# A list scheduler sets the order of four engines in a fused attention and FFN kernel

## The chip, the core and the metric

The kernel runs on one core of one Trainium2 chip. The metric is the device time of one execution in microseconds (us). Every engine of the core (TensorE or PE, VectorE or DVE, ScalarE or ACT, GpSimd or POOL, and SyncE or SP, which issues transfers) takes its own instructions strictly in the order in which the program holds them; an instruction that waits for a semaphore holds back all that stand behind it on that engine.

## The reference

Attention with a threshold, then a bilinear feed-forward layer on its output. The float32 inputs q, k, v have 8 batches, 8 heads, 576 rows and 64 columns. The three weight matrices arrive as float64.

```python
scores = scale * np.matmul(q, k.transpose(0, 1, 3, 2))
thresh = np.max(scores, axis=-1, keepdims=True) - tau
scores = np.where(scores >= thresh, scores, -1000000000.0)
scores = scores - np.max(scores, axis=-1, keepdims=True)
attn = np.exp(scores)
attn = attn / (np.sum(attn, axis=-1, keepdims=True) + 1e-09)
out = np.matmul(attn, v)
...
a = x @ w_a        # x: 4608 x 512, from out; w_a, w_b: 512 x 1536
b = x @ w_b
return a * b @ w_out   # w_out: 1536 x 512
```

## The kernel before

**Tiling.** The work of attention is cut into 144 units, each of 128 rows of queries for a pair of heads. One unit does the following. `scores` (L404) makes two score tiles `sc` of 128x576 in PSUM on PE. On DVE two maxima `mx` (L411) and the threshold `thr` (L412) follow; ACT makes `bias` (L431) and the exponentials `tw` (L432); DVE cuts at the threshold and sums (L435), then takes the reciprocal (L446, L448); ACT scales (`normalise`, L454). The weights are then transposed. In the first 8 units (`BY_PE`) that is done on PE (L479, copied out by ACT L481 and DVE L482); later DVE transposes 32x32 blocks (L498 in `turn_blocks`, two instructions of 128x576 for a unit) and two transfers through DRAM (`swap`) put the blocks in place (`wT`). `product` (L542) multiplies with v into `pv`, and ACT L549 and DVE L550 copy that to the tiles `xT` of x, which POOL also copies with swapped halves (`xS`, L565).

The FFN works on blocks of 256 rows of x: products with `w_a` and `w_b` (`pab`, L824 and L720, partly by Strassen's seven products of sums and differences), their elementwise product `h`, sums of `h` on POOL (L853) and the products with `w_out` (`po`, L885; in the first block L935).

All PSUM tiles (`tp`, `sc`, `pv`, `pab`, `po`) come from one pool of 4 buffers, each of two banks.

**Weights.** In the first 140 us the float64 weights are loaded in 36 pieces (L271, SP's queue) and converted by integer steps: ACT L298 and L299, POOL L305, DVE L311 and L319, POOL L324. A piece's L311 is also the last to read the raw buffer, so that another piece can be loaded to it.

**What sets the order.** The Python text interleaves all of this: the loop over `g` (one unit each) calls `scores`, then the conversion of two or three pieces in portions (`convert_first`, `convert_rest`), `turn_blocks` of the unit before, `weigh`, `weighted`, and between them `advance`, which runs the FFN's matmuls for so many columns as a pace allows. `keep_order` then chains every engine's instructions in just this text order, by a dependency of each on the one before it (reason "order").

The transfers on SP are spread by `pump` and `load_weights`: a transfer waits for the PE instruction that stood last in the text when it was issued (reason "pace").

Of the kernel before, what the change touches and what calls it, by code (L numbers as in the profile page):

```python
# [35 lines left out]
TW_BUFS = 3  # L36
SEVENS = 2
BY_HEAD = 16


def keep_order(tc):

    last = {}
    for ins in tc.nc.cur_bb.bb.instructions:
        before = last.get(ins.engine)
        if before is not None:
            tc.add_manual_dep(
                ins, before,
                mybir.DependencyInfo(mybir.DependencyClass.NoSync, mybir.DependencyReason.DATA),
                reason="order")  # L50
        last[ins.engine] = ins.name


@with_exitstack
def kernel(
# [59 lines left out]
    INV_SCALE = math.sqrt(D)  # L115
    BIG = 3.0e38

    def pool(name, bufs, **kw):
        return ctx.enter_context(tc.tile_pool(name=name, bufs=bufs, **kw))

    const = pool("const", 1)
    loads = pool("loads", 3)
    work = pool("work", 2)
    small = pool("small", 2)
    scratch = pool("scratch", 5, space=bass.MemoryType.DRAM)
    psum = pool("psum", 4, space=PSUM)
# [37 lines left out]
    def flush(*keys):  # L164

        while any(key in keys for key, _, _ in bulk):
            pump(1, False)

    def passed(columns):

        running["pump"] += columns
        while bulk and running["pump"] >= 0:
            running["pump"] -= PUMP * sum(math.prod(to.shape) for to, _ in bulk[0][2]) // PART
            pump()
        if not bulk:
            running["pump"] = min(running["pump"], 0)
# [77 lines left out]
    def load_weights(limit, engine=nc.sync, most=NPIECES):  # L254

        behind = None
        if most < NPIECES:
            behind = next(x.name for x in reversed(nc.cur_bb.bb.instructions) if x.engine == mybir.EngineType.PE)
        while most and (len(raws) - len(taken) < limit or extra) and state["loaded"] < state["due"]:
            most -= 1  # L260
            n = state["loaded"]
            if len(raws) - len(taken) < limit:
                raw = work.tile([P, CW, 2], U32, tag="xT", bufs=XT_BUFS, name="raw")
            else:
                raw = taken[n] = extra.pop(0)
# [12 lines left out]
            state["loaded"] = n + 1  # L278
# [53 lines left out]
    for _ in range(TW_BUFS):  # L332
        t = work.tile([P, 2 * NB, Q], FP32, tag="tw", bufs=TW_BUFS, name="rows")
# [34 lines left out]
    def prep_pe(i, name):  # L368

        m = loaded[i][name]  # L370
        if name == "q":
            mT = first_sb[:, i * S:(i + 1) * S]
        else:
            mT = work.tile([P, S], FP32, tag="kT", bufs=HP, name="kT")
        tp = banks(SH, "tp")
        for c in range(2):
            for n in range(NR // 2):
                nc.tensor.transpose(tp[:, c, n * R:(n + 1) * R], m[:, c * (NR // 2) + n], ident[0:R, 0:R])
        prepared.setdefault(i, {})[name] = mT
        return mT, tp  # L380
# [8 lines left out]
    def scores(i, u):  # L389
# [566 lines left out]
    def store(n):  # L956

        for _ in range(n):
            post("out", pending.pop(0))
# [75 lines left out]
    first = {i: g for g, (i, u) in enumerate(units) if u == 0}  # L1035
# [3 lines left out]
    kT, tp = prep_pe(0, "k")  # L1039
# [17 lines left out]
    n = 0  # L1057
    for g in range(NPIECES):
        size = min(3 if 4 <= g < 10 else 2, NPIECES - n)
        early[g] = list(range(n, n + size))  # L1060
        n += size
    for g in range(len(units) + PV_LAG):
        written = len(pending)
        state["slot"], state["paced"] = g, g > 36
        while bulk and bulk[0][1] < g - 1:
            pump()
# [5 lines left out]
        if BY_PE + 1 < g <= len(units) + 1:  # L1072
            n = g - PV_LAG
# [152 lines left out]
```

## Time and profile before

| | |
|---|---|
| median of 3 runs | 1419.35 us (1418.83 to 1419.81) |
| span of the profiled execution | 1417.0 us |
| PE busy | 1370.2 us (97%) |
| DVE busy | 1013.7 us (72%) |
| ACT busy | 679.9 us (48%) |
| POOL busy | 495.7 us (35%) |
| longest chain | PE 86%, DVE 7%, DMA 3%, issue 2% |

The span goes from the first to the last instruction of the profiled execution; a time also holds what lies around the span. No time of the profiled execution itself is given beside its span, so the median stands for it: 2.35 us lie around the span. "Busy" is the union of an engine's instructions. Matmuls are pipelined, and one that has begun overlaps those that follow, so a busy PE may still wait a little.

### The profile page before, as it was taken

How to read it: one execution, taken by the hardware profiler on the slowest of the kernel's cores; microseconds unless marked ns; L12 is line 12 of the kernel's file. 1: busy time of each engine (PE TensorE's matmuls, PEld its weight loads, DVE VectorE, ACT ScalarE, POOL GpSimd, SP SyncE). 2: the span in 40 equal slices, each digit the busy share in tenths (PEclk: the TensorE clock that was granted, in tenths of full speed). 3: DMA queues.
4: the chain of work that ended last, by engine and by line, in shares of the span. 5: the costliest groups of instructions: out<-in, count | busy, mean ns of one | idle time of the engine just before them, and what ended most of it. 6: DMA issues, size and time to landing. Idle time of an engine off the chain costs nothing.

```text
span 1417.0 us, 76257 instructions
## 1 busy us (share of the span) xinstructions
PE 1370.2 (97%) x33836; PEld 1229.6 (87%) x33836; DVE 1013.7 (72%) x2200; ACT 679.9 (48%) x1245; POOL 495.7 (35%) x678
## 2 busy tenths in 40 slices
PE   6788999999999999999999999999999999999998
PEld 5677579989878887979998999999888899799997
DVE  6898986778777877776767777677777776744424
ACT  5786554545445454545444545454545455431110
POOL 2674541606060606042333324150606060608100
PEclk9999999999999999999999999999999999999999
DMA  9967776667756775666555675567655775550000
GB/s 212 235 193 219 182 214 163 178 153 183 198 135 173 198 188 155 178 156 184 142 134 149 168 193 158 144 160 199 168 144 152 191 201 154 135 152 18 4 19 18
DMA packets 327000, 223.20 MB, mean 158 GB/s; under 512 B 171536, under 2 KB 310800, under 8 KB 326672
## 3 DMA queue, kind: packets, MB, share of 16 engines
q1 hardware_dynamic: 323712, 216.95, 59.2%
q8 instruction: 266, 4.36, 1.3%
q10 hardware_dynamic: 2960, 1.38, 0.4%
q14 instruction: 62, 0.51, 0.1%
HBM read 128.58 MB, written 89.65 MB: 154 GB/s over the span
## 4 chain that ended last, share of the span: by engine, by line
PE 86%; DVE 7%; DMA 3%; issue 2%; SPq 1%; ACT 0%; POOL 0%; DVEq 0%; POOLq 0%; ACTq 0%
PE pab L720 29%; PE po L885 20%; PE pab L824 16%; PE pv L542 10%; PE sc L404 10%; DVE mx L411 2%; DVE tw L498 2%; SPq L144 1%; DMA wT<-swap 1%; DVE tw L435 1%; PE tp L479 1%; DMA raw<-in_moe_w_a_dram 1%; DMA raw<-in_moe_w_b_dram 1%; DVE thr L412 0%; DVE u L790 0%
## 5 line engine op out<-in xcount | busy, mean ns | idle before, releaser
L411 DVE TENSOR_REDUCE mx<-sc 128x1 f32<-128x576 f32 x288 | 204.7, 752 | 125.8 <-PE sc L404 125.4
L454 ACT ACTIVATE tw<-tw,rcp 128x576 f32<-128x576 f32 x272 | 196.5, 770 | 202.3 <-DVE rcp L448 202.3
L682 POOL TENSOR_TENSOR h<-h,u 128x512 f32<-128x512 f32 x28 | 35.2, 1276 | 601.0 <-DVE h L794 426.1
L432 ACT ACTIVATE tw<-sc,bias,scalars 128x576 f32<-128x576 f32 x288 | 239.8, 833 | 10.9 <-PE pab L720 0.4
L435 DVE SCALAR_TENSOR_TENSOR tw<-sc,thr,tw 128x576 f32<-128x576 f32 x288 | 221.5, 799 | 10.4 <-ACT tw L432 9.9
L885 PE MATMUL po<-wo_sb,h 64*64 64x256 f32 x3264 | 205.8, 376 | 1.2 <-DVE h L794 1.1
L498 DVE STREAM_TRANSPOSE tw<-tw 128x576 f32<-128x576 f32 x272 | 194.4, 752 | 0.8 <-ACT tw L454 0.8
L885 PEld LDWEIGHTS po<-wo_sb,h 64*64 64x64 f32 x3264 | 157.0, 133 | 25.7 <-DVE h L794 2.6
L542 PE MATMUL pv<-wT,vm 64*64 64x160 f32 (+3 forms) x5184 | 169.2, 275 | 7.6 <-issue 3.6
L542 PEld LDWEIGHTS pv<-wT,vm 64*64 64x64 f32 x5184 | 157.4, 136 | 19.1 <-issue 9.8
L404 PE MATMUL sc<-kT,qT 64*64 64x288 f32 x2016 | 168.0, 404 | 1.1 <-DVE xt L550 0.5
L853 POOL TENSOR_TENSOR h<-h 128x256 f32<-128x256 f32 x168 | 117.4, 732 | 107.4 <-PE po L885 97.2
L885 PE MATMUL po<-sums_u,h 64*64 64x256 f32 x2448 | 153.4, 376 | 0.7 <-DVE h L832 0.7
L720 PE MATMUL pab<-xU,wb_sb 64*64 64x128 f32 x4352 | 138.0, 269 | 0.4 <-issue 0.3
L720 PEld LDWEIGHTS pab<-xU,wb_sb 64*64 64x64 f32 x4352 | 132.2, 133 | 3.7 <-issue 1.1
L885 PEld LDWEIGHTS po<-sums_u,h 64*64 64x64 f32 x2448 | 117.6, 133 | 19.4 <-DVE h L832 1.3
L404 PEld LDWEIGHTS sc<-kT,qT 64*64 64x64 f32 x2016 | 101.8, 133 | 22.6 <-issue 5.0
L549 ACT COPY xT<-pv 128x128 f32<-128x128 f32 (+1 forms) x68 | 17.7, 260 | 201.8 <-PE pv L542 200.2
L431 ACT ACTIVATE bias<-mx,scalars 128x1 f32<-128x1 f32 x288 | 83.1, 288 | 64.0 <-DVE mx L411 63.7
L550 DVE COPY xT<-pv 64x128 f32<-64x128 f32 (+1 forms) x136 | 38.1, 280 | 91.0 <-PE pv L542 89.7
L720 PE MATMUL pab<-xS,wa_sb 64*64 64x128 f32 x2176 | 101.8, 269 | 0.1
L531 ACT COPY kept<-po 128x512 f32<-128x512 f32 x65 | 34.8, 536 | 123.0 <-PE po L885 113.9
(156 smaller groups left out, 2414.3 us busy)
## 6 DMA issues: line engine op xcount, KB each, us to landing
wT<-swap SPq DMA_DIRECT2D x244, 288.0 KB, 3.9
swap<-tw SPq DMA_DIRECT2D x480, 144.0 KB, 2.9
vm<-in_v_dram SPq DMA_DIRECT2D x128, 72.0 KB, 2.5
swap<-tw SPq DMA_DIRECT2D x128, 72.0 KB, 3.0
kT<-in_k_dram SPq DMA_DIRECT2D x112, 72.0 KB, 3.3
wT<-swap SPq DMA_DIRECT2D x56, 144.0 KB, 3.3
out_dram<-kept SPq DMA_DIRECT2D x28, 256.0 KB, 3.9
qT<-in_q_dram SPq DMA_DIRECT2D x112, 40.0 KB, 2.8
```

The source lines that it names most:

```text
L404: nc.tensor.matmul(sc[m][o * D:o * D + wide, c], qT[r, q0:q0 + wide], kT[r, c * SH:(c + 1) * SH], start=True, stop=True)
L411: nc.vector.tensor_reduce(mx[:, c], sc[j], axis=AX.XY, op=ALU.max)
L431: nc.scalar.activation(bias[:, j:j + 1], mx[:, j:j + 1], AF.Copy, scale=e_nscale)
L432: nc.scalar.activation(wb[j], sb[j], AF.Exp, bias=bias[:, j:j + 1], scale=e_scale)
L435: nc.vector.scalar_tensor_tensor(out=wv, in0=sb[j], scalar=thr[:, j:j + 1], in1=wv, op0=ALU.is_ge, op1=ALU.mult, accum_out=sums[:, j:j + 1])
L454: nc.scalar.activation(w, w, AF.Copy, scale=rcp[:, j:j + 1])
L498: nc.vector.transpose(w, w)
L542: nc.tensor.matmul(pv[c * D:(c + 1) * D, y], vm[rows, s], wT[y](rows, s), start=(s == 0), stop=(s == NSLOT - 1))
L720: nc.tensor.matmul(out[c * D:(c + 1) * D, r, f * P:(f + 1) * P], w[g][k][rows, w0:w0 + D], moving[k][rows], start=(fresh and k == 0 and f ...
L824: nc.tensor.matmul(pab[c:c + columns(), r], w[rows, f // n, k, fs + c:fs + c + columns()], moving, start=(k == 0), stop=(k == H - 1))
L853: (nc.vector if state["over"] else nc.gpsimd).tensor_tensor(*a, **kw)
L885: nc.tensor.matmul(po[c * D:(c + 1) * D, r, y], ht[rows, t0:t0 + D], other[rows, f], start=(f == 0), stop=(f == NF // 2 - 1))
```

## The change

`keep_order` goes, and `order` takes its place, called at the same place with the whole list of instructions. It finds which instruction needs which (from the tiles and areas that they read and write), gives each a cost from its engine and shape, and then walks through a modelled time: at each step it takes, of all engines, the instruction that can start first. An engine may take an instruction ahead of others of its own only among the next `LOOK` of the text: 300 on PE, 24 on DVE and ACT, 12 on POOL. Of those ready at the same time it takes the first of the text. SP looks 1 ahead, so that transfers keep their order. Tiles of a pool are still opened in text order. The order found is then chained as before. `Book` notes the pool and buffers of each tile; the two "pace" dependencies are noted in `after_of` for the model and otherwise unchanged. No instruction of work is added, removed or changed.

In the built programs the four orders differ so. On PE 164 of 16942 matmuls stand at another place (none by more than 80), on DVE 1416 of 1912, on ACT 486 of 1253, on POOL 598 of 681; the 1488 transfers of SP stand as they stood.

```diff
--- before.py
+++ after.py
@@ -1,3 +1,4 @@
+import bisect
 import math
 import struct
 from contextlib import ExitStack
@@ -36,19 +37,241 @@
 TW_BUFS = 3
 SEVENS = 2
 BY_HEAD = 16
-
-
-def keep_order(tc):
-
-    last = {}
-    for ins in tc.nc.cur_bb.bb.instructions:
-        before = last.get(ins.engine)
-        if before is not None:
+LOOK = {mybir.EngineType.PE: 300, mybir.EngineType.DVE: 24, mybir.EngineType.Activation: 24, mybir.EngineType.Pool: 12, mybir.EngineType.SP: 1}
+
+
+BANKS = ("tp", "sc", "pv", "pab", "po")
+class Book:
+
+    def __init__(self, pool, bufs, slots):
+        self.pool, self.bufs, self.slots = pool, bufs, slots
+
+    def tile(self, shape, dtype, **kw):
+        t = self.pool.tile(shape, dtype, **kw)
+        tag = kw.get("tag") or kw["name"]
+        self.slots[t.tensor.name] = (id(self.pool), tag), kw.get("bufs", self.bufs)
+        return t
+
+
+def area(ap):
+
+    name, offset, dims = ap.tensor.name, ap.offset, [(s, n) for s, n in ap.ap]
+    stride, parts = dims[0]
+    lines, first = range(offset // stride // 32, (offset // stride + parts - 1) // 32 + 1), offset % stride
...
+    return name, sum(1 << q for q in lines), mask
+
+
+def stretch(ap):
+
+    return ap.tensor.name, 1, ((1 << (sum(s * (n - 1) for s, n in ap.ap) // 288 + 1)) - 1) << (ap.offset // 288)
+
+
+def spent(ins, outs, x, psum):
+
+    def size(a):
+        return math.prod(n for _, n in a.ap[1:])
+
+    n = max(size(a) for a in ins + outs)
+    e, kind = x.engine, type(x).__name__
+    if e == mybir.EngineType.Activation:
+        if kind == "InstActivation":
+            takes = 240 + 0.86 * n + 45 * (len(ins) - 1)
+            return (takes - 100 if n > 8 else takes, takes)
+        return (80 + 0.83 * n, 165 + 0.83 * n)
+    if e == mybir.EngineType.Pool:
+        return (140 + 2.13 * n, 180 + 2.13 * n) if len(ins) > 1 else (395, 400) if n <= 256 else (580, 615)
+    if len(ins) > 1 and n > 8:
+        more = 75 if len(ins) > 2 else 0
+        return (60 + 1.06 * n + more, 130 + 1.06 * n + more)
+    if n <= 8:
+        return (170, 170 + 60 * (len(ins) > 1))
+    return (75 + 1.04 * n, 150 + 1.04 * n)
+
+
+EARLY = 130e3
+
+
+def order(tc, slots, paced, look):
+
+    PE, SP = mybir.EngineType.PE, mybir.EngineType.SP
+    work = [x for x in tc.nc.cur_bb.bb.instructions]
+    index = {x.name: n for n, x in enumerate(work)}
+    engines = {}
+    uses, after, missing = {}, [[] for _ in work], [0] * len(work)
...
+    for n, x in enumerate(work):
+        engines.setdefault(x.engine, []).append(n)
+        ins, outs, before, behind = [], [], set(), set()
...
+            if name in slots and name.split("_")[0] in BANKS:
+                lines, mask = 15, 1
+                if (name, x.engine) in last and last[name, x.engine] != n:
+                    behind.add(last[name, x.engine])
+                last[name, x.engine] = n
...
+        for m in paced.get(x.name, ()):
+            before.add(index[m])
+        for m in before | behind:
+            after[m].append((n, m in before))
+        missing[n] = len(before | behind)
+        if x.engine == PE:
+            (rows, cols), (r0, c0) = x.tile_size, x.tile_position
+            width = math.prod(k for _, k in outs[0].ap[1:])
+            cost.append((2 * max(2 * width / 2.4 + (4 if width <= 128 else 1 if max(rows, cols) <= 64 else 7), 103), 163))
+            spots[n] = [(r, c) for r in range(r0 // 32, -(-(r0 + rows) // 32)) for c in range(c0 // 32, -(-(c0 + cols) // 32))]
+        elif not ins and not outs:
+            cost.append((0, 0))
+        elif type(x).__name__ == "InstDMACopy":
...
+            total = math.prod(c for _, c in outs[0].ap)
+            piece = min(run(outs[0]), run(ins[0])) * 4
+            cost.append((550, total * 4 / piece * (6 + 0.055 * piece) / 16))
+        else:
+            cost.append(spent(ins, outs, x, any(a.tensor.name.split("_")[0] in BANKS for a in ins)))
...
+    given = dict.fromkeys(free, 0)
...
+    def room(n):
+        at = 0.0
+        for name in opens[n] or ():
+            tag, _ = slots[name]
+            if given[tag] != turn_of[name] or not free[tag]:
+                return None
+            at = max(at, free[tag][0])
+        return at
+
+    while left:
+        best = None
+        for e, some in waiting.items():
+            if not some:
+                continue
+            mine = engines[e]
+            while ahead[e] < len(mine) and done[mine[ahead[e]]]:
+                ahead[e] += 1
+            limit = mine[min(ahead[e] + look[e], len(mine)) - 1]
+            pick = None
+            for n in some:
+                if n > limit:
+                    break
+                at = room(n)
+                if at is None:
+                    continue
+                at = max(at, ready[n], now[e])
+                if pick is None or at < pick[0]:
+                    pick = at, n, e
+                    if at <= now[e]:
+                        break
+            if pick and (best is None or pick[0] < best[0]):
+                best = pick
+        at, n, e = best
+        waiting[e].remove(n)
+        done[n] = True
+        left -= 1
+        result[e].append(n)
...
+        busy, takes = cost[n]
+        if e == PE:
+            at = max([at] + [busy_till.get(z, 0.0) for z in spots[n]])
+            for z in spots[n]:
+                busy_till[z] = at + busy
+            takes += busy
+            busy = 42
+        elif at < EARLY:
+            busy, takes = busy * 1.1, takes * 1.1
+        now[e] = at + busy
+        if type(work[n]).__name__ == "InstDMACopy":
+            dma = max(dma, at + 1100) + takes
+            end = dma + 900
+        else:
+            end = at + takes
+        ended[n] = end
...
+        for m, whole in after[n]:
+            same = not whole or work[m].engine == e and e != SP and type(work[n]).__name__ != "InstDMACopy"
+            ready[m] = max(ready[m], (at + busy if same else end + 60))
+            missing[m] -= 1
+            if not missing[m]:
+                bisect.insort(waiting[work[m].engine], m)
+    for e, some in result.items():
+        for m, n in zip(some, some[1:]):
             tc.add_manual_dep(
-                ins, before,
+                work[n], work[m].name,
                 mybir.DependencyInfo(mybir.DependencyClass.NoSync, mybir.DependencyReason.DATA),
                 reason="order")
-        last[ins.engine] = ins.name
 
 
 @with_exitstack
@@ -115,8 +338,11 @@
     INV_SCALE = math.sqrt(D)
     BIG = 3.0e38
 
+    slots, after_of = {}, {}
+
     def pool(name, bufs, **kw):
-        return ctx.enter_context(tc.tile_pool(name=name, bufs=bufs, **kw))
+        return Book(ctx.enter_context(tc.tile_pool(name=name, bufs=bufs, **kw)), bufs, slots)
+
 
     const = pool("const", 1)
     loads = pool("loads", 3)
@@ -156,6 +382,7 @@
             for n, move in enumerate(bulk.pop(0)[2]):
                 moved = nc.sync.dma_start(*move)
                 if n == 0 and paced:
+                    after_of.setdefault(moved.ins.name, []).append(behind)
                     tc.add_manual_dep(
                         moved.ins, behind,
                         mybir.DependencyInfo(mybir.DependencyClass.Sync, mybir.DependencyReason.DATA),
@@ -270,6 +497,7 @@
                     dst = dst.rearrange("p (k f) -> p k f", k=2)
                 moved = engine.dma_start(dst, part)
                 if behind and r == 0:
+                    after_of.setdefault(moved.ins.name, []).append(behind)
                     tc.add_manual_dep(
                         moved.ins, behind,
                         mybir.DependencyInfo(mybir.DependencyClass.Sync, mybir.DependencyReason.DATA),
@@ -1190,7 +1418,7 @@
     while complete or blocks or running["ffn"] is not None:
         advance(DM)
         store(len(pending))
-    keep_order(tc)
+    order(tc, slots, after_of, LOOK)
 
 
 # ---- launch: one core; inputs and outputs as the reference has them ----
```

More of the change, by code (lines that the diff above doesn't have):

```diff
@@ new lines, in area @@
+def area(ap):
+    name, offset, dims = ap.tensor.name, ap.offset, [(s, n) for s, n in ap.ap]
+    stride, parts = dims[0]
+    lines, first = range(offset // stride // 32, (offset // stride + parts - 1) // 32 + 1), offset % stride
+    mask, unit = 0, 1 << max(0, (stride // 144).bit_length() - 1)
+    starts = [first]
+    inner = dims[1:]
+    while inner and len(starts) * inner[0][1] <= 64 and len(inner) > 1:
+        starts = [z + k * inner[0][0] for z in starts for k in range(inner[0][1])]
+        inner = inner[1:]
+    reach = sum(s * (n - 1) for s, n in inner)
+    for z in starts:
+        lo, hi = z // unit, (z + reach) // unit
+        mask |= ((1 << (hi - lo + 1)) - 1) << lo
+    return name, sum(1 << q for q in lines), mask
@@ new lines, with run @@
+EARLY = 130e3
[5 more added lines that the diff above has]
+    uses, after, missing = {}, [[] for _ in work], [0] * len(work)
+    cost, opens, tile_left, of_tile = [], [None] * len(work), {}, [() for _ in work]
+    line, last, spots, busy_till = {}, {}, {}, {}
+    for n, x in enumerate(work):
+        engines.setdefault(x.engine, []).append(n)
+        ins, outs, before, behind = [], [], set(), set()
+        for what, into in ((x.ins, ins), (x.outs, outs)):
+            for a in what:
+                a = getattr(a, "bass_ap", None)
+                if a is not None:
+                    into.append(a)
+        names = set()
+        for a, write in [(a, False) for a in ins] + [(a, True) for a in outs]:
+            name = a.tensor.name
+            dram = name not in slots
+            if dram and not name.startswith("swap"):
+                continue
+            _, lines, mask = (stretch if name.startswith("swap") else area)(a)
+            past = uses.setdefault(name, [])
+            if name in slots and name not in line:
+                line[name] = n
+                opens[n] = (opens[n] or ()) + (name,)
+            if name in slots and line[name] != n:
+                behind.add(line[name])
+            names.add(name)
+            if name in slots and name.split("_")[0] in BANKS:
[3 more added lines that the diff above has]
+                last[name, x.engine] = n
+            kept = []
+            for use in past:
+                m, w, l, k = use
+                hit = l & lines and k & mask
+                if hit and (w or write) and m != n:
+                    (behind if mask == 1 and x.engine == work[m].engine == PE else before).add(m)
+                if not (write and hit and l | lines == lines and k | mask == mask and m != n):
+                    kept.append(use)
+            if not (write is False and past and past[-1] == (n, False, lines, mask)):
+                kept.append((n, write, lines, mask))
+            uses[name] = kept
+        for name in names:
+            if name in slots:
+                tile_left[name] = tile_left.get(name, 0) + 1
+        of_tile[n] = tuple(t for t in names if t in slots)
+        for m in paced.get(x.name, ()):
[11 more added lines that the diff above has]
+        elif type(x).__name__ == "InstDMACopy":
+            def run(a):
+                k = 1
+                for s, c in reversed([*a.ap[1:]] if a.tensor.name in slots else [*a.ap]):
+                    if s == k:
+                        k *= c
+                    elif c > 1:
+                        break
+                return k
+            total = math.prod(c for _, c in outs[0].ap)
[3 more added lines that the diff above has]
+            cost.append(spent(ins, outs, x, any(a.tensor.name.split("_")[0] in BANKS for a in ins)))
+    opened, free, turn_of = {}, {}, {}
+    for n, names in enumerate(opens):
+        for name in names or ():
+            tag, bufs = slots[name]
+            turn_of[name] = opened.get(tag, 0)
+            opened[tag] = opened.get(tag, 0) + 1
+            free.setdefault(tag, [0.0] * bufs)
+    given = dict.fromkeys(free, 0)
+    ready, ended = [0.0] * len(work), [0.0] * len(work)
+    ahead = {e: 0 for e in engines}
+    done = [False] * len(work)
+    waiting = {e: [] for e in engines}
+    now = {e: 0.0 for e in engines}
+    gone = {}
+    result = {e: [] for e in engines}
+    for n, k in enumerate(missing):
+        if not k:
+            bisect.insort(waiting[work[n].engine], n)
+    dma, left = 0.0, len(work)
+    def room(n):
[21 more added lines that the diff above has]
+                if at is None:
+                    continue
+                at = max(at, ready[n], now[e])
+                if pick is None or at < pick[0]:
+                    pick = at, n, e
+                    if at <= now[e]:
+                        break
+            if pick and (best is None or pick[0] < best[0]):
[5 more added lines that the diff above has]
+        result[e].append(n)
+        for name in opens[n] or ():
+            tag, _ = slots[name]
+            given[tag] += 1
+            free[tag].pop(0)
+        busy, takes = cost[n]
[14 more added lines that the diff above has]
+        ended[n] = end
+        for name in of_tile[n]:
+            gone[name] = max(gone.get(name, 0.0), end)
+            tile_left[name] -= 1
+            if not tile_left[name]:
+                bisect.insort(free[slots[name][0]], gone[name])
+        for m, whole in after[n]:
[6 more added lines that the diff above has]
+        for m, n in zip(some, some[1:]):
```

## The prediction

> **What bounds the kernel now.** I first cut the span into five stages. In the rows of this view stand, behind the stage and its length, the busy time of PE, PEld, DVE, ACT and POOL, the granted clock, the share of the DMA engines and GB/s.
>
> ```profile
> 0.00:20.00 20.00, 10.95 (x56) 8.11 (x58) 8.36 (x22) 8.21 (x15) 1.93 (x8) 1.00 1.07 204
> 20.00:142.00 122.00, 100.97 (x1834) 89.04 (x1832) 109.00 (x241) 94.83 (x193) 73.71 (x83) 0.94 0.89 216
> 142.00:205.00 63.00, 61.48 (x1078) 40.64 (x1078) 57.65 (x124) 34.59 (x66) 34.99 (x26) 1.00 0.76 189
> 205.00:1381.00 1176.00, 1167.15 (x30147) 1063.70 (x30142) 822.89 (x1785) 540.50 (x971) 383.38 (x560) 1.00 0.58 153
> 1381.00:1417.00 36.00, 29.64 (x747) 28.06 (x738) 15.76 (x31) 1.76 (x3) 1.68 (x2) 0.94 0.06 17
> ```
>
> From 205 to 1381 us PE is busy for 1167.15 of 1176 us: this stage is PE's own work, and an order that removes no matmul can gain at most the 8.85 us that are left. From 20 to 142 us it is otherwise: PE idles 122 - 101.0 = 21.0 us, and DVE, with 109.0 of 122 us, is the busiest engine. That is the stage in which units of attention and conversions of weights share DVE, and there the change can gain most. In it the DMA engines are also nearly full (0.89).
>
> Next I asked what DVE waited for between 20 and 142 us (total, times, longest):
>
> ```profile
> DVE mx L411 <- PE sc L404: 3.1, 6, 0.9
> DVE xt L550 <- PE pv L542: 3.0, 2, 1.5
> DVE rcp L448 <- ACT sums L444: 1.9, 3, 1.0
> DVE xT L550 <- PE pv L542: 1.6, 2, 1.4
> DVE h L832 <- PE pab L824: 1.0, 1, 1.0
> ```
>
> These are waits at the head of a queue in text order; what stands behind is often ready. DVE's timeline shows the largest such hole:
>
> ```profile
> 14.83 0.74 DVE L383 COPY kT<-tp 128x576 f32<-128x576 f32 x1
> 17.94 1.42 DVE L411 TENSOR_REDUCE mx<-sc 128x1 f32<-128x576 f32 x2 [2.38 <-PE sc L404]
> ...
> 20.20 0.68 DVE L311 SCALAR_TENSOR_TENSOR low<-raw,low 128x512 uint32<-128x512 uint32 x1
> 20.80 0.42 DVE L319 TENSOR_SCALAR wa_sb<-wa_sb 128x512 uint32<-128x512 uint32 x1
> ```
>
> DVE waits 2.38 us for scores, and then does an L311 whose input ACT had ready at 13.88 + 0.67 = 14.55 us.
>
> **The change, part by part.** I compared the two built programs engine by engine. No work is added, so every term is time gained or lost in waits. SP's order is the same. The count of semaphore waits differs by under 3% on every engine, so I cost it at nothing.
>
> *Holes of 15 to 25 us.* L311, L319 and another L311 now stand ahead of this `mx`: 0.68 + 0.42 + 0.68 = 1.8 us of work in a hole of 2.38, and in the next unit L311 and L319 (1.1 us) ahead of a hole of 0.45. Far bound: a gain of 2.9 us. But the next weights set a rail. The chain of waits has the seventh piece's second half under way from 25.69 us for 8.49 us, so that it lands at 34.18:
>
> ```profile
> 25.69 8.49 DMA raw<-in_moe_w_a_dram
> ```
>
> In the new order ACT's L298 and L299 of that piece stand ahead of the fourth unit's `bias`, which ACT began at 34.65 us:
>
> ```profile
> 34.65 0.30 ACT L431 ACTIVATE bias<-mx,scalars 128x1 f32<-128x1 f32 x1
> ```
>
> The pair takes 0.68 + 0.67 us less an overlap of about 0.1, so `bias` begins no earlier than 35.4: 0.75 us later than before, whatever was gained ahead of it. The DMA engines are full there (1.05 to 1.2 in each stretch of 10 us up to 65), so the piece can't land earlier. Between a gain of 2.9 and a loss of 0.75 I take a gain of 0.5: the unit is held, but DVE has two steps of conversion behind it.
>
> *Holes of 66 to 78 us.* DVE waits 0.93 us (`mx`), 1.43 (`xT`) and 1.00 (`h`). Ahead of these now stand L311 and L319 (1.1), L311 (0.68), and L311 and L319 (1.1), whose pieces landed at 55 us and later: 0.93 + 0.68 + 1.00 = 2.6 us filled. The units after it show almost no idle DVE, so this should reach the end of the stage; part of it will meet PE's own loop instead. Far bounds 0 and -3.4; I take -1.5.
>
> *Holes of 127 to 132 us.* PE waits 2.93 us for `wT` to come back from DRAM, and DVE behind it 1.45 + 1.53 us for `xt`, then 1.04 for the sums. The new order puts three L311, two L319 and a reciprocal (2.9 us) ahead of those copies. PE's wait stays, since `wT` is issued behind the same PE instruction. Bounds 0 and -4.0; I take -2.
>
> *From 142 to 205 us* DVE idles 5.35 us but PE only 1.5: I take -1.0.
>
> *PE's own order.* Eight matmuls of `pab` now go ahead of a transpose that waited 1.13 us ("issue", at 62.58): -0.5. Against it, at two places eight `sc` matmuls, which went round all four quarters of the array, now do one half of the rows and then the other. Sixteen rows of 64x288 took about 1.0 us; with half of the array in use they take up to twice that. Bounds 0 and +2.0; I take +1.0.
>
> *The long stage.* Here most of DVE's moves lie: of 272 block transposes L498, 254 now stand ahead of a maximum that they followed, and 190 of 200 copies L550 stand later. What covers this is slack. From the starts and ends in the trace, a score tile's bank has been read out 2.9 us (median; 1.5 at the tenth percentile) before PE needs the bank used four tiles later, a `pv` bank 6.3 us (least 1.7). Two L498 take 1.43 us, a `pv` copy is put off by some 2.5 us (two small operations, a transpose of 0.49 to 0.75 and the L498 pair). So PE should feel little. Bounds: -8.85, all of PE's idle time, to +10, the price of the slower rival below; I take -0.5.
>
> *The end* (6.4 us idle in the last 36) is a chain with the same order in both: 0.
>
> Sum: -0.5 - 1.5 - 2.0 - 1.0 - 0.5 + 1.0 - 0.5 = **-5.0 us**. The profiled span is 1417.0 us, 2.35 under the median; that difference should stay, so 1417.0 - 5.0 + 2.35 = 1414.35, given as **1414.4 us**.
>
> **The rivals.**
>
> *The wait moves on (no change).* Weights land on a rail and PE's order is nearly the text's, so a DVE that is free sooner only waits elsewhere: nearly every hole of the early stage begins with PE or DMA. For it: the 34.18 us landing above, and PE's 2.93 us for `wT`. Against: from the twelfth piece on, weights land 3 to 19 us before ACT converts them, and units 9 to 12 leave DVE no idle time. Then only the last four small terms stay: about 1419.
>
> *Static order, late partner (slower).* Place: L498 ahead of `mx` from 205 us on. L498 needs ACT's `normalise` L454. In the old timeline L454 ended, in the median of 136 units, 0.5 us after `mx` had begun. So `mx`, and with it the release of the score bank, can be held for up to 0.5 + 1.43 us or more. It decides where this is over the bank's slack, 1.5 us in the worst tenth. If one unit in ten of some 120 loses 0.6 us, that is +7 us: 1426; if one in seven, +10. Against it: DVE waited 113.4 us for these scores in this stage, so the transposes mostly fit in that wait.
>
> *The clock stays up (faster still).* The granted clock was half in three stretches of the early stage (the clock is the number behind POOL's):
>
> ```profile
> 47.40:50.80 3.40, 3.40 (x75) 3.28 (x76) 3.11 (x8) 3.02 (x8) 3.07 (x5) 0.50 1.07 238
> 71.30:74.70 3.40, 3.40 (x34) 3.07 (x32) 3.33 (x10) 2.96 (x6) 2.18 (x3) 0.50 0.80 242
> 125.90:132.70 6.80, 5.93 (x154) 5.54 (x155) 2.75 (x11) 1.94 (x7) 0.79 (x2) 0.50 0.77 202
> ```
>
> If tighter work kept it whole, up to half of 13.6 us, 6.8, would come on top: 1407.6. Against it: the waits ahead of these stretches, 1.83 us of PE at 68 and 2.93 at 124, are not among those that the order of PE changes.
>
> The Trainium skill ("TensorE: Matmul & The Clock Gate", section "What's actually happening") has the clock gated to half after an idle window of about 3.4 us. The lengths of 3.4, 3.4 and 6.8 us agree with such a window. Its section "HAM oscillation" asks for no idle gaps over about 3.4 us; the waits named above are shorter and the clock fell all the same, so the trace does not bear that threshold out. By that threshold this rival would gain nothing.
>
> **How the numbers follow.** Forecast (1410 to 1416.5): 0.42. Faster still (1402 to 1410), with the clock or more of the holes: 0.16. No change (within 0.2%, 2.8 us, about what a measurement of this kernel can tell from none): 0.24. Slower (1422 to 1432): 0.18. So faster 0.58, same 0.24, slower 0.18. The range of 8 in 10 runs from 1404, most of the faster case, to 1425, where about half of the slower case is left out.
>
> **What would show it.** Right: in the changed profile DVE's waits for `mx`, `xT` and `h` before 142 us shrink (8.7 us in the list above, the sums' wait left out, to about 4), the stage up to 205 us ends some 5 us earlier (the same FFN matmul begins earlier), and PE's idle time from there to the last stage stays at 8 to 9 us. Wrong: DVE or ACT waits for `raw` transfers between 30 and 60 us (the wait moved on); PE's wait for score banks (`sc` or `pab` released by DVE L435) appears in the long stage; or half-clock stretches of other number or length.

## The result

The changed kernel is slower: median 1442.55 us (1437.57 to 1445.98, 4 runs) against 1419.58, a ratio of 1.0145 with a 95% interval of 1.0126 to 1.0163. The profiled execution took 1442.91 us with a span of 1441.1, 24.1 us over the span before. The forecast was 1414.4.

On POOL far fewer instructions moved than the section on the change says (598 of 681). The profiles have 678 instructions there, and by line, tiles and shape 155 of them stand at another place; tiles of one name are not told apart in this count, so it is a lower bound. Nothing was worked out from that number.

Old line numbers are used in the text; the profile of the changed kernel counts its own (most are 228 higher: L365 is L593 there, L411 L639, L435 L663, L498 L726; in e6, e9, e10 and e13 another 6).

The profile after, by stages (length, busy time of PE, PEld, DVE, ACT and POOL, granted clock, DMA share, GB/s). The last two stages are moved by the 24 us:

```profile
0.00:20.00 20.00, 11.00 (x66) 8.27 (x68) 10.42 (x26) 8.46 (x16) 3.56 (x9) 0.91 1.07 199
20.00:142.00 122.00, 102.58 (x1846) 90.00 (x1844) 114.97 (x241) 95.07 (x194) 79.36 (x88) 0.96 0.89 219
142.00:205.00 63.00, 55.91 (x960) 39.83 (x960) 55.04 (x110) 31.49 (x59) 30.19 (x20) 0.92 0.72 182
205.00:1405.00 1200.00, 1178.15 (x30232) 1089.79 (x30228) 857.30 (x1793) 542.88 (x975) 381.99 (x560) 1.00 0.57 150
1405.00:1441.00 36.00, 29.77 (x759) 26.56 (x750) 16.90 (x33) 1.75 (x3) 1.68 (x2) 0.98 0.06 17
```

Against the table in the prediction, the early stage has changed little (PE +1.6 us). From 142 to 205 us PE idles 7.1 us instead of 1.5, and in the long stage 1200 - 1178.15 = 21.9 instead of 8.85. To place the loss in time, I took the end of the last maximum `mx` of each unit, which is a mark on the same work in both (units are counted from 0): the changed kernel is 0.7 us ahead at unit 12 (115 us), 5.3 us behind at unit 24 (210 us), 7.6 at unit 66, 18.5 at unit 120 and 23.4 at the last, unit 143. So it creeps in over the whole long stage.

Between the marks of units 24 and 143, before and after, with almost the same number of matmuls:

```profile
209.80:1250.50 1040.70, 1031.96 (x26218) 929.77 (x26214) 772.11 (x1696) 518.30 (x932) 348.23 (x518) 1.00 0.64 167
215.10:1273.90 1058.80, 1037.67 (x26227) 956.14 (x26221) 800.93 (x1695) 518.94 (x933) 348.77 (x522) 1.00 0.62 163
```

Of the 18.1 us that this stretch is longer, 12.4 are idle time of PE (21.1 us instead of 8.7). In the other 5.7 PE is busy for longer on the same work; no run shows why.

DVE's waits in the long stage, before (205 to 1381 us) and after (205 to 1405 us), as total, times and longest:

```profile
DVE mx L411 <- PE sc L404: 113.4, 94, 4.4
...
DVE qT L365 <- DMA qT<-in_q_dram: 6.4, 5, 2.2
```

```profile
DVE tw L726 <- ACT tw L682: 79.2, 104, 1.6
DVE mx L639 <- PE sc L632: 52.5, 69, 1.9
...
DVE kT L593 <- DMA kT<-in_k_dram: 28.9, 16, 3.8
DVE qT L593 <- DMA qT<-in_q_dram: 28.0, 27, 3.0
```

Two new waits show. The transposes of the weights (L498, here L726) wait 79.2 us for ACT's `normalise`: the place of the slower rival. And DVE's transposes of k and q (L365, here L593) wait 57 us for their transfers, a wait that the prediction had not looked at: 67 of these 84 stand earlier, by up to 18 places, and 47 of them ahead of a cut L435 that they followed. One such place, on DVE:

```profile
1118.10 0.17 DVE L676 RECIPROCAL rcp<-sums 128x2 f32<-128x2 f32 x1
1121.94 0.78 DVE L593 STREAM_TRANSPOSE kT<-kT 128x576 f32<-128x576 f32 x1 [3.68 <-DMA kT<-in_k_dram]
1122.64 1.40 DVE L726 STREAM_TRANSPOSE tw<-tw 128x576 f32<-128x576 f32 x2
1123.96 1.39 DVE L639 TENSOR_REDUCE mx<-sc 128x1 f32<-128x576 f32 x2
...
1125.91 0.82 DVE L663 SCALAR_TENSOR_TENSOR tw<-sc,thr,tw 128x576 f32<-128x576 f32 x1 [0.30 <-ACT tw L660]
```

and on SP (the issue of that k) and PE:

```profile
1114.07 3.52 SPq L383 DMA_DIRECT2D kT<-in_k_dram  x4
```

```profile
1117.94 1.18 PE L632 MATMUL sc<-kT,qT 64*64 64x288 f32 x16
...
1126.79 1.43 PE L770 MATMUL pv<-wT,vm 64*64 64x160 f32 x33 [1.79 <-DVE tw L663]
```

The scores were done at 1117.94 + 1.18 = 1119.1 us, and DVE was free from 1118.3. But k was issued until 1117.6 and its transpose could begin only at 1121.94. With the pair L498 behind it (1.40 us) it held the maximum, whose scores it has no part in, until 1123.96, and the cut L435 until 1125.91. PE waited 1.79 us for that cut.

### The profile page after: what moved, and what is told of

Same layout as the page of the kernel before. It is cut to its first block, busy times and chain, and to the rows that moved or that the text cites. A ratio compares the mean times of both kernels' runs of the same rounds, so it can differ in the third digit from the quotient of the medians.

```text
span 1441.1 us, 76274 instructions
## 1 busy us (share of the span) xinstructions
PE 1377.4 (96%) x33836; PEld 1254.4 (87%) x33836; DVE 1054.6 (73%) x2200; ACT 679.7 (47%) x1245; POOL 496.8 (34%) x678
## 3 DMA queue, kind: packets, MB, share of 16 engines
q10 hardware_dynamic: 2960, 1.38, 0.4%
## 4 chain that ended last, share of the span: by engine, by line
PE 81%; DVE 9%; DMA 4%; issue 2%; ACT 2%; SPq 2%; POOL 0%; POOLq 0%; DVEq 0%; ACTq 0%
PE pab L948 27%; PE po L1113 19%; PE pab L1052 16%; PE sc L632 9%; PE pv L770 8%; DVE tw L663 2%; DVE tw L726 1%; DMA qT<-in_q_dram 1%; DVE mx L639 1%; SPq L383 1%; PE po L1163 1%; DVE low L539 1%; DMA raw<-in_moe_w_b_dram 1%; DMA vm<-in_v_dram 1%; ACT tw L660 0%
## 5 line engine op out<-in xcount | busy, mean ns | idle before, releaser
L663 DVE SCALAR_TENSOR_TENSOR tw<-sc,thr,tw 128x576 f32<-128x576 f32 x288 | 230.5, 810 | 39.4 <-ACT tw L660 33.4
L726 DVE STREAM_TRANSPOSE tw<-tw 128x576 f32<-128x576 f32 x272 | 198.5, 761 | 82.0 <-ACT tw L682 81.6
L639 DVE TENSOR_REDUCE mx<-sc 128x1 f32<-128x576 f32 x288 | 203.9, 748 | 62.8 <-PE sc L632 61.8
L1113 PE MATMUL po<-wo_sb,h 64*64 64x256 f32 x3264 | 215.1, 376 | 1.7 <-DVE tw L663 1.7
L632 PE MATMUL sc<-kT,qT 64*64 64x288 f32 x2016 | 187.7, 407 | 10.2 <-DVE xt L778 5.0
L1113 PEld LDWEIGHTS po<-wo_sb,h 64*64 64x64 f32 x3264 | 162.4, 133 | 25.3 <-issue 2.1
L1113 PE MATMUL po<-sums_u,h 64*64 64x256 f32 x2448 | 162.8, 376 | 0.4 <-DVE h L1081 0.4
L632 PEld LDWEIGHTS sc<-kT,qT 64*64 64x64 f32 x2016 | 114.1, 133 | 32.1 <-issue 7.0
L948 PE MATMUL pab<-xS,wa_sb 64*64 64x128 f32 x2176 | 111.2, 269 | 0.7 <-issue 0.7
L1052 PE MATMUL pab<-xS,wa_sb 64*64 64x256 f32 (+2 forms) x1248 | 96.6, 368 | 0.0
L948 PE MATMUL pab<-xT,wa_sb 64*64 64x128 f32 x1856 | 93.2, 270 | 1.7 <-DVE tw L663 0.9
L948 PEld LDWEIGHTS pab<-xS,wa_sb 64*64 64x64 f32 x2176 | 91.7, 133 | 1.7 <-issue 1.0
```

What stands on the lines that cost most here:

```text
L632: nc.tensor.matmul(sc[m][o * D:o * D + wide, c], qT[r, q0:q0 + wide], kT[r, c * SH:(c + 1) * SH], start=True, stop=True)
L639: nc.vector.tensor_reduce(mx[:, c], sc[j], axis=AX.XY, op=ALU.max)
L663: nc.vector.scalar_tensor_tensor(out=wv, in0=sb[j], scalar=thr[:, j:j + 1], in1=wv, op0=ALU.is_ge, op1=ALU.mult, accum_out=sums[:, j:j + 1])
L726: nc.vector.transpose(w, w)
L948: nc.tensor.matmul(out[c * D:(c + 1) * D, r, f * P:(f + 1) * P], w[g][k][rows, w0:w0 + D], moving[k][rows], start=(fresh and k == 0 and f ...
L1052: nc.tensor.matmul(pab[c:c + columns(), r], w[rows, f // n, k, fs + c:fs + c + columns()], moving, start=(k == 0), stop=(k == H - 1))
```

## The experiments

Theory A is the slower rival: L498 ahead of `mx` waits for ACT and holds it. Theory B: L365 set ahead waits for its transfer and holds DVE's queue. Theory C: the loss lies in the orders of the other engines (ACT, POOL and PE). The table gives each ratio to the kernel before with its 95% interval, and from each profile DVE's waits ended by a transfer of q or k, and the waits of L498 for ACT.

| run | ratio | q, k waits, us | L498 for ACT, us |
|---|---|---|---|
| before | 1 | 7.8 | 0.8 |
| the change | 1.0145 (1.0126 to 1.0163) | 57.6 | 81.6 |
| e1 DVE in text order | 1.0027 (1.0004 to 1.0050) | 10.4 | 2.0 |
| e2 only DVE scheduled | 1.0123 (1.0092 to 1.0154) | 61.6 | 60.1 |
| e3 change, L365 held | 1.0028 (1.0011 to 1.0046) | 11.9 | 92.9 |
| e4 change, L498 held | 1.0087 (1.0054 to 1.0119) | 41.5 | 0.8 |
| e5 change, both held | 1.0048 (1.0030 to 1.0066) | 7.0 | 0.8 |
| e6 text, L365 free | 1.0038 (1.0012 to 1.0065) | 37.2 | 0.8 |
| e7 change, later landings in the model | 1.0018 (1.0000 to 1.0036) | 5.5 | 84.3 |
| e8 scheduled up to 145 us only | 1.0021 (0.9996 to 1.0045) | 8.8 | 0.8 |
| e9 text, L498 free | 0.9961 (0.9936 to 0.9985) | 20.1 | 62.5 |
| e10 text, L365 and L498 free | 1.0078 (1.0049 to 1.0106) | 63.4 | 59.0 |
| e11 as e7, PE in text order | 1.0031 (1.0010 to 1.0052) | 5.6 | 84.0 |
| e12 as e7, only DVE scheduled | 1.0009 (0.9989 to 1.0029) | 14.0 | 62.4 |
| e13 as e10, later landings in the model | 0.9957 (0.9939 to 0.9975) | 6.2 | 63.9 |
| e14 as e2, L365 held | 1.0009 (0.9993 to 1.0025) | 19.9 | 62.8 |
| e15 scheduled from 145 us only | 1.0132 (1.0103 to 1.0160) | 61.9 | 80.7 |
| e16 as e8, then L498 free | 0.9986 (0.9965 to 1.0008) | 27.4 | 63.0 |
| e17 as e12, from 145 us only | 0.9979 (0.9955 to 1.0003) | 14.2 | 63.1 |
| e18 as e7, from 145 us only | 0.9990 (0.9967 to 1.0012) | 4.7 | 82.4 |

The chips differed, and on some the kernel before itself ranged by over 1%; so ratios are compared, not times.

**Which engine.** e1 sets one look to 1, e2 the other three.

```diff
-LOOK = {mybir.EngineType.PE: 300, mybir.EngineType.DVE: 24, mybir.EngineType.Activation: 24, mybir.EngineType.Pool: 12, mybir.EngineType.SP: 1}
+LOOK = {mybir.EngineType.PE: 300, mybir.EngineType.DVE: 1, mybir.EngineType.Activation: 24, mybir.EngineType.Pool: 12, mybir.EngineType.SP: 1}
```

> The scheduler as in the change, but VectorE may look only 1 ahead, so that it keeps its text order; TensorE, ScalarE and GpSimd are still reordered. Theories A (the block transposes of the weights, set ahead of the maxima, wait for ScalarE) and B (the transposes of q and k, set ahead, wait for their transfers) both put the loss on VectorE's queue: about 1420 us. Theory C (the orders of the other engines, such as score matmuls by halves of the array): about 1435 to 1442.

```diff
-LOOK = {mybir.EngineType.PE: 300, mybir.EngineType.DVE: 24, mybir.EngineType.Activation: 24, mybir.EngineType.Pool: 12, mybir.EngineType.SP: 1}
+LOOK = {mybir.EngineType.PE: 1, mybir.EngineType.DVE: 24, mybir.EngineType.Activation: 1, mybir.EngineType.Pool: 1, mybir.EngineType.SP: 1}
```

> Only VectorE is scheduled; TensorE, ScalarE and GpSimd keep the text order. If nearly all of the loss comes from VectorE's order: about 1440 on a chip where the kernel before takes 1420 (ratio 1.012 to 1.015). If the other engines' orders cost some of it: ratio 1.008 to 1.012.

The ratios 1.0027 and 1.0123 say that nearly all of the loss is DVE's order. C is out but for a rest of some 0.2%.

**Which of DVE's moves.** In e3, e4 and e5 a kind of transpose stays behind the 24 DVE instructions that precede it in the text, by a dependency added in `order`:

```diff
         for m in paced.get(x.name, ()):
             before.add(index[m])
+        if x.engine == mybir.EngineType.DVE and type(x).__name__ == 'InstStreamTranspose' and outs[0].tensor.name[:2] in ('kT', 'qT'):
+            behind.update(engines[x.engine][-25:-1])
+            behind -= before
```

> As the change, but VectorE's transposes of q and k (old line L365) may not pass any of the 24 instructions of VectorE that precede them in the text. A: the loss stays, 1435 to 1442. B: most of it goes, 1420 to 1426, and VectorE's wait for the q and k transfers falls from 57 us to about 8. Both at once: about halfway, 1430.

For e4 the tile is `tw`; for e5 both kinds are held.

> As the change, but VectorE's transposes of the weights (old line L498) may not pass any of the 24 instructions of VectorE that precede them in the text. A: most of the loss goes, 1420 to 1426, and the wait of these transposes for ScalarE falls from 82 us to a few. B: the loss stays, 1435 to 1442. Both at once: about halfway, 1430.

> As the change, but neither kind of VectorE's transposes (old lines L365, L498) may pass the 24 instructions of VectorE that precede it. A or B or both: 1414 to 1420, since the gain of some 2 us up to 142 us stays. C: 1435 or more.

Holding L365 takes the ratio from 1.0145 to 1.0028, with the waits of L498 for ACT still there (92.9 us). That speaks for B and against A. But holding L498 also helped (1.0087); the q and k waits fell with it, to 41.5 us, so e4 does not part the two. e5 is no better than e3, although in e3 248 of the 272 L498 still stand ahead of a maximum that they followed and in e5 none: moving L498 costs nothing in the changed kernel either. The 1.0048 of e5 also lies above the 1414 to 1420 us expected for it: the early gain that was counted on there does not show (e8, below).

**Each move alone.** In e6, e9 and e10 the looks are those of e2, and all is in text order but for the transposes named (of `kT` and `qT`, of `tw`, of all three), which may go ahead by up to 24. The edit of e9:

```diff
-    engines = {}
+    engines, free_ones = {}, set()
...
+        if x.engine == mybir.EngineType.DVE:
+            if type(x).__name__ == 'InstStreamTranspose' and outs[0].tensor.name[:2] == 'tw':
+                free_ones.add(n)
+            else:
+                behind.update(m for m in engines[x.engine][-25:-1] if m not in free_ones)
+                behind -= before
```

> Everything in text order, but VectorE's transposes of q and k (old line L365) may go ahead by up to 24. B (these transposes wait for their transfers and hold VectorE's queue): ratio 1.008 to 1.012, with some 40 us of waits for q and k transfers on VectorE. If they do harm only together with the early transposes of the weights: 1.000 to 1.004.

> Everything in text order, but VectorE's transposes of the weights (old line L498) may go ahead by up to 24; 131 of 272 then stand ahead of the maxima they followed. A (they wait for ScalarE and hold the maxima): ratio 1.004 or more, as many of these waits as fit. B (only waits for transfers hurt; these merely take the place of the maxima's wait for scores): 0.999 to 1.002, with tens of us of waits for ScalarE before them.

> Everything in text order, but both kinds of VectorE's transposes (old lines L365, L498) may go ahead. The transposes of q and k alone gave 1.0038, all of VectorE 1.0123. If the two kinds together make the loss (the weights' transposes let those of q and k come earlier still, 50 ahead of the cut L435 against 29): 1.009 to 1.013. If the copies and other small operations are needed too: 1.003 to 1.007.

e9 decides A: the weights' transposes ahead of the maxima (131 of 272 here) make the kernel **faster**, 0.9961, although they wait 62.5 us for ACT. DVE's waits in its long stage suggest why nothing is lost:

```profile
DVE tw L732 <- ACT tw L688: 60.0, 72, 1.4
...
DVE mx L645 <- PE sc L638: 25.9, 51, 2.1
```

Before, DVE waited 113.4 us for scores at `mx`; now 60.0 us of waiting come first and 25.9 are left, so the one wait stands in the place of the other. With L365 alone free the ratio was 1.0038. That is less than expected of B (1.008 to 1.012) and inside the range of the other case, that L365 does harm only together with L498. With both free it was 1.0078: freeing L498 sends L365 further ahead (50 of 84 in front of a cut L435 that they followed, against 29), and the q and k waits go from 37 to 63 us.

**Taking away the reason, not the freedom.** In the scheduler's model a transfer lands 0.9 us after its data has passed. e7 and e13 make that 3.9, for every transfer; nothing else changes in the scheduler, and L365 may still go ahead.

```diff
-            end = dma + 900
+            end = dma + 3900
```

> As the change, but the scheduler's model lets every transfer land 3 us later. If the harm of B is that the model has transfers land too early: the transposes of q and k take later places, and the ratio is 1.002 to 1.006, as with them held (1.003). If it is the weights' transposes: it stays near 1.0145.

> As the run in which both kinds of VectorE's transposes are free (1.0078), but the model lets every transfer land 3 us later, so that those of q and k take later places. If the loss there is the wait for transfers: back to the gain of the weights' transposes alone (0.996), 0.995 to 0.999, and the q and k waits fall from 63 us to under 20. If it is the displaced order itself: 1.004 or more.

The change comes down from 1.0145 to 1.0018, and e10 from 1.0078 to 0.9957. L365 still goes ahead of its place in the text, 58 times of 84 in e7 and 57 in e13, but ahead of a cut L435 only 17 and 18 times instead of 47 and 50. L498 keeps its moves (252 and 140 ahead of a maximum, against 254 and 141). With e3 and e14, which hold L365 alone, this shows B: the loss comes from L365 set too far ahead. What it does not part is the wait of L365 for its transfer from its own work of some 0.4 to 0.8 us ahead of a cut, since both go when it stands later. That the wait is the larger part is argued from its size, 57 us.

DVE's waits of these transposes in the long stage of e10, and those of e13 (only q's are left):

```profile
DVE kT L599 <- DMA kT<-in_k_dram: 29.5, 18, 3.4
...
DVE qT L599 <- DMA qT<-in_q_dram: 26.5, 26, 2.5
```

```profile
DVE qT L599 <- DMA qT<-in_q_dram: 4.1, 4, 2.2
```

PE gets the time back. Between the marks of units 24 and 143 in e10, and in e13:

```profile
208.70:1263.90 1055.20, 1032.82 (x26226) 959.94 (x26222) 786.38 (x1696) 518.25 (x933) 347.57 (x518) 1.00 0.63 164
206.50:1251.70 1045.20, 1032.87 (x26225) 966.08 (x26221) 788.75 (x1695) 518.35 (x933) 348.20 (x518) 1.00 0.64 166
```

PE is busy for the same time, and its idle time falls from 22.4 to 12.3 us.

**The rest.** e14 is e2 with L365 held as in e3; e11 is e7 with PE's look set to 1, e12 is e7 with all looks but DVE's set to 1, as in e2; e8 and e15 give a look over 1 only to instructions before, or from, text number 1940 (about 145 us); e16 is e8 with L498 alone free from there on, as in e9; e17 and e18 are e12 and e7 with the look from there on only. The edit of e8:

```diff
-            limit = mine[min(ahead[e] + look[e], len(mine)) - 1]
+            early = int(work[mine[ahead[e]]].name[2:]) < 1940
+            limit = mine[min(ahead[e] + (look[e] if early else 1), len(mine)) - 1]
```

> Only VectorE scheduled, its transposes of q and k held behind the 24 instructions before them, with the model's own transfers. If these transposes are the whole loss of VectorE's order (1.0123): 0.996 to 1.000. If the copies of pv and the small operations, which move here too, cost some: 1.001 to 1.004.

> As the run whose model lets transfers land 3 us later (1.0018), and TensorE in text order besides. If the rest of the loss is TensorE's moved matmuls: 0.998 to 1.000. If it is noise or the other engines: 1.001 to 1.003.

> Model with transfers 3 us later, and only VectorE scheduled. If VectorE's order alone is harmless once transfers are not expected too early: 0.998 to 1.002; if it needs the other engines' orders to go with it: 1.004 or more.

> The scheduler sets the order only up to the end of the stage in which weights are converted (about 145 us); from there all engines keep the text order. The changed kernel was 2.3 us ahead there, so if that gain is real and lasts: ratio 0.998 to 0.999, about 2 us faster. If it is eaten by later waits for transfers: 1.000 or a little more.

> Text order up to about 145 us, the change's scheduler from there. If the whole loss is made in the long stage: ratio 1.012 to 1.016, as the change. If the early stage's order loses 5 us of it at the handover: 1.008 to 1.011.

> The scheduler up to about 145 us, then text order with only VectorE's transposes of the weights free. If the early gain of 2 us adds to that of these transposes (0.996): 0.994 to 0.996. If the early order is worth nothing (as the run with it alone, 1.002, has it): 0.996 to 1.000.

> Only VectorE scheduled, only from about 145 us on, and with transfers 3 us later in the model. With the early stage too this gave 1.0009; the two kinds of transposes alone, with such a model, 0.9957. If the early stage's order costs that half per cent: 0.995 to 0.998. If the copies and small operations that move in the long stage cost it: 1.000 to 1.002.

> All four engines scheduled as in the change, but only from about 145 us on and with transfers 3 us later in the model (with the early stage too: 1.0018). If the early stage's order is what costs: 0.995 to 0.999. If it is the orders of TensorE, ScalarE and GpSimd or VectorE's small operations: 1.000 to 1.003.

Where L498 is free, q and k early cost the same in three settings: e13 to e10 1.2%, e12 or e14 to e2 1.1%, e7 or e3 to the change 1.2%. Where L498 stays in the text's place it is 0.4% in two: e5 to e4, and before to e6. e15 has the whole loss without the early order. The early order gains nothing that shows alone (e8, expected at 0.998 to 0.999, or at 1.000 or a little more), and with it left out the versions with later landings come to 0.9979 and 0.9990 instead of 1.0009 and 1.0018; e16 lies above e9 too. That all points to a cost of 0.2 to 0.3%, though each interval overlaps its partner's. PE's moves cost nothing that e11 could show. e9 and e13 are the fastest versions, about 0.4% under the kernel before.

One more rival is settled by the profiles: DVE's own work takes longer in the new order, 857.30 us in the long stage instead of 822.89. That is not the loss, for in e7 it takes 860.18 us (205 to 1386 us) at a ratio of 1.0018.

## Why the prediction was wrong

**The long stage is the step that failed.** The prediction gave it -0.5 us, with a bound of +10; it cost 18 of the 23.4 us (unit 24 to the last). It rested on the moves of L498 and L550 and on the slack of PSUM banks. It named a transpose of 0.49 to 0.75 us beside the pair L498, which by its length can only be L365, and counted that length ahead of a copy; it put the wait of L365 for its transfer at nothing, without a reason. The orders had 67 of 84 set earlier, and the profile before had their transfers at 2.8 us (q) and 3.3 us (k) from issue to landing. That wait came to 57 us, and holding L365 in its place took the ratio from 1.0145 to 1.0028 (e3). A wait of up to 3.8 us at the head of DVE's queue is over the 2.9 us (median) by which a score bank was early. The sign that the prediction had named for this appeared, too: in the long stage PE waited for `pab` and `sc` tiles until DVE's L435 was done, which it did not before.

```profile
PE pab L948 <- DVE tw L663: 0.9, 2, 0.6
...
PE sc L632 <- DVE tw L663: 0.6, 1, 0.6
```

**The slower rival had the sign and not the cause**, and its 1422 to 1432 us was too low. It named L498 held by `normalise`. The wait came (79.2 us in the long stage), but e9 shows no cost of it and a gain of 0.4% from the move. What was set against that rival, that the wait would fit in the 113.4 us of waiting for scores, agrees with e9.

**The early stage, -5.0 in four terms, brought nothing.** The holes were filled in good part: of DVE's waits from 20 to 142 us, those for `mx`, `xT` (with `xt`) and `h` fell from 8.7 to 4.3 us, close to the forecast 4, and the wait of 2.38 us before `mx` fell to 0.37. The waits after:

```profile
DVE mx L639 <- PE sc L632: 3.0, 5, 1.0
DVE low L539 <- ACT low L527: 1.0, 1, 1.0
DVE h L1060 <- PE pab L1052: 1.0, 1, 1.0
DVE xT L778 <- PE pv L770: 0.3, 1, 0.3
```

But DVE's 241 instructions there, as many as before, took 114.97 us instead of 109.0: part of the filled time went into longer instructions (an L311 from `raw` took 937 ns in the mean instead of 710, 3.2 us in all). The rail of the weights held as forecast, and with it came the sign named for no gain: ACT waited 1.41 us for the seventh piece, and the fourth unit's `bias` began at 36.14 us; the prediction had "no earlier than 35.4":

```profile
35.01 0.67 ACT L526 ACTIVATE wa_sb<-raw 128x512 f32<-128x512 f32 x1 [1.41 <-DMA raw<-in_moe_w_a_dram]
35.59 0.66 ACT L527 ACTIVATE low<-raw 128x512 f32<-128x512 uint32 x1
36.14 0.28 ACT L659 ACTIVATE bias<-mx,scalars 128x1 f32<-128x1 f32 x1
```

The handover at 142 to 205 us, forecast at -1.0, lost some 6 us in this profile; e15, without the early order, is only 0.4 us behind at unit 24 and 23.4 at the last (its profile is of another chip), so this is not the cause of the whole.

**PE's own order** (+0.5 in sum) is too small a term for these runs: e11 found no gain in PE's text order, and its interval is 3 us wide on either side. **The end** (0) was right: PE idles 6.2 us of the last 36, as before 6.4. **The clock** was at half for 3.4, 3.4, 3.4, 3.4 and 10.2 us before 205 us, longer than before (3.4, 3.4 and 6.8): that rival failed. The stretch of 10.2 us, from 169.5 us on, follows a chain that ran through DVE and a q transfer at 164 to 170 us. PE waited 1.38 us ahead of it and 2.85 us inside it. The Trainium skill ("TensorE: Matmul & The Clock Gate", "HAM oscillation") asks for no idle gaps over about 3.4 us. These two are shorter and the clock was at half all the same; ahead of the stretch at 108.1 us, though, PE had waited 3.5 us.

**Two small slips in the numbers** change nothing in this. In every run that gives both, 1.8 us lie around the span and not 2.35. And with the last four terms alone the no-change rival comes to 1418.35, not "about 1419".

**Left open.** Why L365 early costs three times as much with L498 free is shown by how often it stands ahead of a cut (47 to 50 of 84 in the change, e2 and e10, against 21 and 29 in e4 and e6) and by the waits (63 against 37 us), but not by a mechanism of its own. Why e9 and e13 gain 0.4% was not traced. And what part of a landing the model has wrong, the issue on SP, the queue or the transfer, was not measured; 3 us more were enough.

## What to carry to other kernels

On an engine that takes its instructions in order, setting an instruction ahead is safe only as far as its partner's lateness is known. A transfer that lands later than a planner believes (DVE waited up to 3.8 us here) stalls everything behind it, also where that engine is busy only 72% of the time. Rank moved instructions by what they wait for, transfers first, not by how many there are: 67 transposes set ahead, among some 1400 moved instructions of DVE, made nearly the whole loss. Waiting time of an engine says little by itself: 60 us of new waits cost nothing where they stand in for an older wait, and 50 us elsewhere came with a loss of 1.2%.

## What the runs showed of the hardware

DVE's small operation L446 (L674 in the changed kernel) works on 128x2 elements. At 154.66 us it took 0.17 us, and 5 us later 2.07, beside an instruction of POOL:

```profile
159.91 2.07 DVE L674 TENSOR_SCALAR sums<-sums 128x2 f32<-128x2 f32 x1
159.59 2.36 POOL L905 TENSOR_TENSOR first_u<-wa_sb,first_u 128x1024 f32<-128x1024 f32 x1
```

The one ended at 161.98 us and the other at 161.95. In this profile 34 of the 136 L446 took over 0.3 us, and each of them ended 22 to 32 ns after a POOL instruction beside it had ended. Most of the others (83 of 102) had no POOL instruction beside them. So an L446 of DVE looks held until POOL's instruction is done. The 10 L311 over 0.8 us and the 10 L319 over 0.6 us also ran beside POOL, but so did 18 and 6 of the shorter ones. Not every DVE instruction is held: a pair L411 at 155.41 us took its usual 1.38 us while POOL was at work. No run took POOL's work away, so what decides it stays open. It is not the main loss either: the mean of L446 rose from 236 to 320 ns in the changed kernel, 11 us of DVE's time in all, and it stood at 289 in e3, whose ratio is 1.0028.
